# Swapped copies of N and Z taken from GpSimd, masks of P ahead of the weight loads, three unread products fewer, in the begin of a DeltaNet and SwiGLU kernel

## The chip, the cores and the metric

One Trainium2 chip, of which the kernel uses one core. A core has TensorE (PE, matrix products), VectorE (DVE), ScalarE (ACT), GpSimd (POOL) and SyncE (SP, which here issues nearly all DMA transfers). Each runs its own instruction list in order and waits on semaphores for the others. TensorE reads SBUF and writes PSUM.

The metric is the time of one execution on the device in microseconds. The time before is the median of three runs.

## What is computed

The reference first runs a recurrence over 768 steps for each of 4 batches and 8 heads (head size 48), and then a SwiGLU block over the 3072 tokens (model size 384, inner size 1536), all in 32-bit floats:

```python
k_n = k / (np.linalg.norm(k, axis=-1, keepdims=True) + 1e-06)
state = np.zeros((B, H, D, D), dtype=np.float32)
for t in range(S):
    kt, vt, bt = (k_n[:, :, t], v[:, :, t], beta[:, :, t, None])
    y[:, :, t] = np.einsum('bhd,bhde->bhe', q[:, :, t], state)
    v_old = np.einsum('bhde,bhd->bhe', state, kt)
    state = state + bt[:, :, :, None] * np.einsum('bhd,bhe->bhde', kt, vt - v_old)
...
x = np.ascontiguousarray(attn_out.transpose(0, 2, 1, 3)).reshape(B * S, H * D)
g = x @ w_gate
silu = g * (1.0 / (1.0 + np.exp(-g)))
val = x @ w_val
return (silu * val @ w_out).astype(np.float32)
```

## The kernel before

**Chunks.** The 768 steps are cut into 12 chunks of 64. Within a chunk the recurrence is solved with matrices: the products of all keys with all keys (`gram_steps`, `first_gram`), the inverse of a triangular matrix built from them, and the products of queries with keys, P, of which a mask keeps one triangle (`under_mask`, L539). Chunk by chunk the state is passed on, and the 256 tokens of a finished chunk go through the SwiGLU block. Arrays over batch and head are split in two by parity of the head (`par`) and two by batch (`b`); each combination has one half of the 128 partitions, 64 rows. `ORDER` (L360) walks through the four combinations, and matrix products of 64x64 are issued for each.

**The begin.** Chunks 0 and 1 are treated apart. Their triangular matrices are cut into blocks of 16 and 32: VectorE inverts the blocks of 16 by substitution (`first_substitution`, L690, 15 steps of two operations), `first_z` turns the result, and `spread_z` (L714) writes it under a row mask into `ztp[0]`, as the matrix Z: its blocks on the diagonal, one call for each chunk and each half x of the columns (columns 0 to 31 and 32 to 63), on the engine that it is given. Z is thus the inverse of the blocks on the diagonal alone. What stands below them is taken in by N: `n_products` (L728) makes N from the low blocks (`l_sb`) and Z in two PSUM banks, one for each parity, and `n_copies` (L738) copies both banks to SBUF (`n_sb`). It then writes a second copy of the odd parity with the two halves of the partitions swapped (`n_back`, L744), since a product needs its two operands on the same partitions. In the kernel before this copy is made on GpSimd, from SBUF to SBUF, in two parts of 64x512.

**The first chunk.** `first_advance` (L939) is a generator that is stepped by hand. Counted as products for the first chunk, all in L950 and in two parts each (bp 0 in the banks `px`, bp 1 in `py`):

1. Z by V, copied to `v` by ScalarE (L975),
2. N by `v`, copied to `uu` (L985),
3. N by `uu`, with `n_back` as the weights for odd parity; VectorE adds it to `v` in `t` (L997), and ScalarE copies the odd half of `t` to the other partitions (L999),
4. N by `t`, added to `t` in `uu` by VectorE (L1009),
5. the masked P (`p_sb`) by `uu`, copied to `y` (L1022 and L1024, bp 0 on ScalarE, bp 1 on VectorE).

Then `y` is turned on TensorE (L1036) and copied to `x_first` (L1037), which the SwiGLU products of chunk 0 read; and `of_state` (L916) makes the state after chunk 0. Chunk 1 does the same in `advance` (L1111) with its own N (`n_products(1)` at L2019), stepped between the SwiGLU products of chunk 0.

**The weights.** w_gate, w_val and w_out come in 42 pieces; pieces 0 to 23 are 128x256 each, alternately of the gate and the value matrix, six for each 256 inner columns. `stage` (L250) issues the load of one on SyncE's queue. To keep few loads in flight, `stage(n, after)` first lets GpSimd copy one column of piece `after` into the place of piece n (L261, called a gate below): the load of n waits for this copy, and the copy for the landing of piece `after`. A staged piece is then converted to the form in which TensorE reads it: two operations on ScalarE (`power_step`, L274 and L280, called the powers of a piece) and three on VectorE (`convert`, L293, L301, L313). The SwiGLU products of the first chunks are in `gate_val` (L1544); their matrix products are L1552.

**The order.** The engines' instruction lists are exactly in the order in which the program issues the instructions (`manual_schedule`, L1908). The order of the begin is written out from L1917 on. What an engine, or SyncE's queue, has earlier in this list it finishes earlier: a gate that waits for a load holds up everything behind it on GpSimd. `unread(n, bank)` (L634) issues n products of constants whose result nobody reads. `first_q[0]` is the generator of P of chunk 0: its first step makes the products, the second copies them to `p_sb` (ScalarE, L521), and the third and fourth mask one parity each on GpSimd (L536).

In the kernel before GpSimd's list from the first loads on is therefore: the gates of pieces 2 to 7, the swapped copies of N of chunk 0, the gates of 8 and 9, the two masks of P, the gates of 10 to 13, `spread_z` of chunk 1 twice (L1981), the gates of 14 to 17, and the swapped copies of N of chunk 1.

Of the kernel before, what the change touches and what calls it, by code (L numbers as in the profile page):

```python
# [20 lines left out]
def kernel(  # L21
# [25 lines left out]
    nc = tc.nc  # L47
# [25 lines left out]
    def ps_pair(name, tag):  # L73

        return pairs_of_banks[tag]
# [58 lines left out]
    def halves(x, c, b):  # L134
        return x[NB * b : NB * b + NB, :, c * C : (c + 1) * C, :]
# [43 lines left out]
    def load_v(c):  # L179
        vin[c] = work.tile([128, 2, NB, NJ, D], FP32, name="vin", bufs=2)  # L180
        for b in range(2):
            src = halves(v, c, b).rearrange("bp (j par) p d -> par p (bp j) d", par=2)
            for par in range(2):
                s = half_of(b ^ par if c > 1 else b).start
                nc.sync.dma_start(  # L185
                    out=vin[c][s : s + 64, par].rearrange("p bp j d -> p (bp j) d"),
                    in_=src[par],
                )
# [174 lines left out]
    def half_of(x):  # L363
        return slice(64 * x, 64 * x + 64)
# [89 lines left out]
    def banks(name, tag):  # L454

        if type(tag) is int:
            return [ps_ffn([128, 512], name, tag + i) for i in range(2)]
        p = ps_pair(name, tag)
        return [p[:, 0], p[:, 1]]
# [141 lines left out]
    first_of, l_sb, n_sb = {}, {}, {}  # L601
# [32 lines left out]
    def unread(count, p):  # L634

        for _ in range(count):
            nc.tensor.matmul(p[0:R], half, half[:, 0:1].to_broadcast([128, 512]))
# [100 lines left out]
    def n_copies(c, p_n, copies, back):  # L738
        for par in range(2):
            copies[par](  # L740
                n_sb[c][:, par].rearrange("p bp j i -> p (bp j i)"), p_n[par]
            )
        for x in range(2):
            back(n_back[c][half_of(x)], n_sb[c][half_of(1 - x), 1].rearrange(  # L744
                "p bp j i -> p (bp j i)"
            ))

    n_back = {}

# [189 lines left out]
    def first_advance():  # L939

        zt = ztp[0][:, 0].rearrange("p (par bp j) i -> p par bp j i", par=2, bp=NB)
        r = vin.pop(0)
        p_n = banks("p_n", 2)
        n_products(0, p_n)
        n_copies(0, p_n, (nc.scalar.copy, nc.vector.tensor_copy), nc.gpsimd.tensor_copy)

        def product(p, at, flip, weights, moving):
            for j in range(NJ):
                for par, b in ORDER:
                    nc.tensor.matmul(  # L950
                        p[half_of(b ^ par if flip else b), at[par], j],
                        weights(par, b, j),
                        moving(par, b, j),
                    )

        def there(par, b):
            return half_of(b ^ par)

        v, uu = new_u("v0"), new_u("uu")
        t = x_flat.rearrange("p (x bp j d) -> p x bp j d", x=3, bp=NB, j=NJ)  # L960
        pairs = [
            ps_pair("p_u", tag)[:, :, 0 : NJ * D].rearrange("p x (j d) -> p x j d", j=NJ)
            for tag in ("px", "py")
        ]
        n_of = n_sb[0]
        back_of = n_back[0].rearrange("p (bp j i) -> p bp j i", bp=NB, j=NJ)
        for bp in range(NB):
            product(
                pairs[bp],
                (1, 0),  # L970
                True,
                lambda par, b, j: zt[half_of(b), par, bp, j],
                lambda par, b, j: r[half_of(b), par, bp, j],
            )
            nc.scalar.copy(v[:, :, bp], pairs[bp])  # L975
        yield MORE
        for bp in range(NB):
            product(
                pairs[bp],
                (0, 1),  # L980
                False,
                lambda par, b, j: n_of[there(par, b), par, bp, j],
                lambda par, b, j: v[there(par, b), 1 - par, bp, j],
            )
            nc.scalar.copy(uu[:, :, bp], pairs[bp])  # L985
        yield MORE
        for bp in range(NB):
            product(
                pairs[bp],
                (1, 0),  # L990
                True,
                lambda par, b, j: (
                    back_of[half_of(b), bp, j] if par else n_of[half_of(b), 0, bp, j]
                ),
                lambda par, b, j: uu[half_of(b), par, bp, j],
            )
            plus(t[:, 0:2, bp], v[:, :, bp], pairs[bp])  # L997
            for x in range(2):
                nc.scalar.copy(t[half_of(x), 2, bp], t[half_of(1 - x), 0, bp])  # L999
        yield MORE  # L1000
        for bp in range(NB):
            product(
                pairs[bp],
                (0, 1),
                False,
                lambda par, b, j: n_of[there(par, b), par, bp, j],
                lambda par, b, j: t[there(par, b), 1 - par, bp, j],
            )
            plus(uu[:, :, bp], t[:, 1:3, bp], pairs[bp])  # L1009
        held_loads[26] = lambda: load_v(2)  # L1010
        yield
        pq = p_sb.pop(0)
        y = work.tile([128, NB, NJ, 2, D], FP32, name="y", tag="r", bufs=2)
        for bp, copy in enumerate((nc.scalar.copy, nc.vector.tensor_copy)):
            product(
                pairs[bp],
                (0, 1),
                True,
                lambda par, b, j: pq[half_of(b), par, bp, j],
                lambda par, b, j: uu[half_of(b), par, bp, j],  # L1020
            )
            copy(y[:, bp, :, 0], pairs[bp][:, 0])  # L1022
            for b in range(2):
                copy(y[half_of(b), bp, :, 1], pairs[bp][half_of(1 - b), 1])  # L1024
        yield
        y_f = y.rearrange("p bp j par d -> p bp (j par d)")
        xts[0] = x_first
        p_f = [
            p[:, 0 : KT * 128].rearrange("p (t n) -> p t n", t=KT)
            for p in banks("p_f", 2)  # L1030
        ]
        x_v = x_first.rearrange("p t (bp n) -> p t bp n", bp=NB)
        for bp, copy in enumerate((nc.scalar.copy, nc.vector.tensor_copy)):
            for k in range(KT):
                at = slice(k * 128, (k + 1) * 128)
                nc.tensor.transpose(p_f[bp][:, k], y_f[:, bp, at], ident)  # L1036
            copy(x_v[:, :, bp], p_f[bp])  # L1037
        yield
        p_s = of_state(0, uu)
        nc.scalar.copy(state, p_s)  # L1040
        yield
# [581 lines left out]
    def plus(out, a, b):  # L1623
        nc.vector.tensor_tensor(out=out, in0=a, in1=b, op=ALU.add)  # L1624
# [283 lines left out]
    with tc.manual_schedule(  # L1908
# [18 lines left out]
        copy_a = nc.scalar.copy  # L1927
# [14 lines left out]
        for n in range(6):  # L1942
            stage(n, n - 2 if n > 1 else None)
        load_v(1)
        unread(2, banks("p_t", "py")[0])
        turned(2, False, "py")
        first_q = [gram_steps(0, True, 0, (copy_a, copy_a))]
        next(first_q[0])
        gram(2, False, "px", (copy_a, copy_a))
        turned(3, False, "py")  # L1950
        unread(1, banks("p_t", 2)[0])
        turned(1, True, "px")
        gram(3, False, "py", (copy_a, copy_a))
        first_q.append(gram_steps(1, True, "px", (copy_a, copy_a)))
        next(first_q[1])
        next(first_q[0])
        unread(4, banks("p_t", 2)[0])
        first_substitution()
        first_z()
        some, others = slice(0, 1), slice(1, NB)  # L1960
# [4 lines left out]
        scale_v(0)  # L1965
        next(first_q[1])
        stage(6, 4)
        stage(7, 5)
        zb_1 = work.tile([128, R, R], FP32, name="zb", bufs=1)
        new_nt(0, spare_of_q, state_flat[:, LEAD : LEAD + 512])  # L1970
        new_nt(1, zb_1.rearrange("p k i -> p (k i)"), spare_of_q[:, 0:512])
        gens["advance", (0,)] = [first_advance(), 0]
        step("advance", advance, 0)
        for n in (8, 9):
            stage(n, n - 2)
        next(first_q[0])
        next(first_q[0])
        for n in range(10, 14):
            stage(n, n - 3)
        for x in range(2):  # L1980
            spread_z(1, x, nc.gpsimd)  # L1981
        for n in range(14, 23):
            stage(n, n - 3 if n < 18 else None)
        power_step(0)
        step("advance", advance, 0)
        converts_first(0)
# [18 lines left out]
        def chain(_):  # L2005

            at = len(went)
            went.append(1)
            n, ahead = (1, 2, 4, 1, 2, 1, 2, 1, 2, 1, 2, 1)[at], (7, 6, 4, 4)[min(at, 3)]
            if n:  # L2010
                convert(todo[:n], ahead)
                del todo[:n]
            if at in chain_at:
                if at in chain_at[4:6]:
                    next(first_q[1])
                if at == 0:
                    step("advance", advance, 0)
                    p_n = banks("p_n", 2)
                    n_products(1, p_n)  # L2019
                    n_copies(1, p_n, (copy_a, copy_a), nc.gpsimd.tensor_copy)  # L2020
                else:
                    step("advance", advance, 1)

# [74 lines left out]
```

## Time and profile before

| | |
|---|---|
| median of three runs | 671.86 us (670.39 to 671.89) |
| the profiled execution's own time | 672.2 us |
| its span, first to last instruction | 670.5 us |
| TensorE busy (page, part 1) | 651.4 us, 97% |
| VectorE, ScalarE, GpSimd busy | 476.7, 279.1, 208.0 us |
| mean granted clock of TensorE | 0.987 |

The page's part 1 gives busy times and part 2 the span in 40 slices. The timeline lists instructions with start and length in us from the start of the span, merges equal ones that follow each other (x64), and shows in brackets how long the engine stood idle before and what released it. TensorE's instructions overlap in a pipeline, so that lengths of merged rows can overlap. The table of stretches gives busy times, instructions and the granted clock in any cut of the span; the clock is 1.00 or 0.50, and a value between them is a stretch that holds a change. "PEld" is the loading of weights into TensorE, "issue" is time in which an engine waited for nothing that the profile shows.

Some rows of GpSimd and VectorE that the change touches, from the groups by line of the first 60 us:

| operation | mean of one |
|---|---|
| L744 POOL copy 64x512, SBUF to SBUF | 610 ns |
| L740 ACT copy 128x512 from PSUM | 586 ns |
| L740 DVE copy 128x512 from PSUM | 691 ns |
| L540 POOL mask 128x512 | 1350 ns |
| L726 POOL spread of Z 128x512 | 2054 ns |
| L726 DVE spread of Z 128x256 | 437 ns |
| L724 ACT spread of Z 128x256 | 742 ns |

### The profile page before, as it was taken

To read this page: it belongs to the slowest core of one execution; us is meant where nothing else is said; L and a number is where in the kernel's file an instruction comes from. 1 tells how busy PE (TensorE), PEld (TensorE's weight loads), DVE (VectorE), ACT (ScalarE), POOL (GpSimd) and SP (SyncE) were. 2 spreads that over 40 slices of the span, in tenths; PEclk is the share of its full clock that TensorE was granted. 3 is DMA by queue.
4 is the path that set the end of the run, shared out by engine and by line. 5 is a ranking of instruction groups with operands and counts; after the bars stand their busy time and mean duration, and the time that the engine had idled before them with its cause. 6 is when DMAs were issued, how large, how long until landed. Compare 5 with 4: busy or idle time off the path is not lost.

```text
span 670.5 us, 24923 instructions
## 1 busy us (share of the span) xinstructions
PE 651.4 (97%) x10854; PEld 598.6 (89%) x10854; DVE 476.7 (71%) x989; ACT 279.1 (42%) x622; POOL 208.0 (31%) x316
## 2 busy tenths in 40 slices
PE   8859999999999999999999999999999999999997
PEld 4548888856899999999999999999999999999997
DVE  6748979899968867858766857766848655655562
ACT  5646776505432642342542442542332532433330
POOL 7052050105697030883030883030883000000000
PEclk9968999999999999999999999999999999999999
DMA  9565757002861262176364175254164342132221
GB/s 135 128 181 177 239 94 218 2 12 32 250 106 50 47 138 81 31 146 158 64 134 116 28 142 142 63 122 104 35 148 107 79 107 80 52 93 72 73 79 24
DMA packets 147438, 68.57 MB, mean 102 GB/s; under 512 B 123456, under 2 KB 126560, under 8 KB 147328
## 3 DMA queue, kind: packets, MB, share of 16 engines
q1 hardware_dynamic: 144992, 66.48, 41.7%
q8 instruction: 85, 1.39, 0.9%
q10 hardware_dynamic: 2080, 0.39, 0.4%
q0 software_dynamic: 256, 0.10, 0.1%
q14 instruction: 25, 0.20, 0.1%
HBM read 59.08 MB, written 7.86 MB: 100 GB/s over the span
## 4 chain that ended last, share of the span: by engine, by line
PE 83%; DVE 6%; DMA 4%; SPq 3%; ACT 2%; issue 2%; POOL 0%; DVEq 0%; ACTq 0%; POOLq 0%
PE ffn L1397 39%; PE ffn L1671 20%; PE ffn L1581 4%; PE ffn L1552 4%; DMA h_f<-in_moe_w_val_dram 2%; PE p_px L1159 2%; PE p_px L920 2%; SPq L139 1%; PE p_py L1061 1%; PE p_px L1142 1%; PE p_py L501 1%; PE p_py L1078 1%; PE p_px L501 1%; SPq L185 1%; PE p_py L902 1%
## 5 line engine op out<-in xcount | busy, mean ns | idle before, releaser
L1397 PE MATMUL ffn<-x_t,w_gv 128*128 128x128 f32 x800 | 108.7, 279 | 0.8 <-DVE p_sb L1621 0.8
L1397 PEld LDWEIGHTS ffn<-x_t,w_gv 128*128 128x128 f32 x800 | 97.4, 192 | 3.6 <-DVE p_sb L1621 1.3
L1431 ACT ACTIVATE sil<-ffn 128x256 f32<-128x256 f32 x100 | 36.5, 383 | 115.8 <-PE ffn L1397 108.9
L1397 PE MATMUL ffn<-x_ffn,w_gv 128*128 128x128 f32 x640 | 84.6, 275 | 0.0
L1671 PE MATMUL ffn<-wo_sb,h_f 128*128 128x192 f32 x480 | 83.9, 328 | 0.0
L819 POOL TENSOR_TENSOR n_b<-mb,half 128x32 f32<-128x32 f32 x5 | 30.4, 6073 | 161.1 <-DVE mb L555 161.1
L1671 PEld LDWEIGHTS ffn<-wo_sb,h_f 128*128 128x128 f32 x480 | 77.9, 190 | 0.6
L1397 PEld LDWEIGHTS ffn<-x_ffn,w_gv 128*128 128x128 f32 x640 | 78.0, 192 | 0.3
L586 POOL TENSOR_TENSOR h_f<-zb,mb 128x31 f32<-128x31 f32 (+15 forms) x124 | 70.7, 570 | 19.2 <-DVE mb L575 9.7
L592 POOL TENSOR_TENSOR zb<-zb,h_f 128x31 f32<-128x31 f32 (+15 forms) x124 | 70.1, 565 | 9.7
L1397 PE MATMUL ffn<-x_t,h_f 128*128 128x128 f32 x472 | 64.9, 280 | 0.7 <-DMA h_f<-w_s 0.4
L1397 PEld LDWEIGHTS ffn<-x_t,h_f 128*128 128x128 f32 x472 | 57.3, 192 | 2.7 <-issue 0.5
L1432 DVE TENSOR_TENSOR h_f<-sil,ffn 128x256 f32<-128x256 f32 x100 | 39.3, 417 | 23.2 <-ACT sil L1431 23.2
L1093 ACT COPY x_ffn<-p_py 32x256 f32<-32x256 f32 (+3 forms) x108 | 39.4, 365 | 29.1 <-PE p_py L1078 27.3
L1621 DVE TENSOR_TENSOR ffn<-p_sb,ffn 128x512 f32<-128x512 f32 x40 | 27.9, 696 | 27.4 <-PE ffn L1397 26.7
L1624 DVE TENSOR_TENSOR ffn<-ffn,p_sb 128x512 f32<-128x512 f32 x40 | 27.2, 689 | 16.0 <-PE ffn L1397 16.0
L1552 PE MATMUL ffn<-x_t,w_gv 128*128 128x256 f32 x144 | 35.4, 397 | 0.9 <-ACT w_gv L274 0.7
L1671 PE MATMUL ffn<-last_k,h_f 128*128 128x192 f32 x200 | 36.0, 327 | 0.0
L1624 DVE TENSOR_TENSOR o_sb<-o_sb,ffn 128x192 f32<-128x192 f32 x50 | 17.5, 350 | 24.1 <-PE ffn L1671 23.5
L1671 PEld LDWEIGHTS ffn<-last_k,h_f 128*128 128x128 f32 x200 | 32.9, 190 | 0.1
L1552 PEld LDWEIGHTS ffn<-x_t,w_gv 128*128 128x128 f32 x144 | 27.2, 195 | 5.7 <-ACT w_gv L274 1.1
L1552 PE MATMUL ffn<-x_ffn,w_gv 128*128 128x256 f32 x144 | 31.9, 380 | 0.0
(330 smaller groups left out, 1184.5 us busy)
## 6 DMA issues: line engine op xcount, KB each, us to landing
h_f<-w_s SPq DMA_DIRECT2D x81, 256.0 KB, 2.9
more_w<-w_s SPq DMA_DIRECT2D x27, 256.0 KB, 2.7
vin<-in_v_dram SPq DMA_DIRECT2D x48, 96.0 KB, 3.4
out_dram<-o_sb SPq DMA_DIRECT2D x48, 96.0 KB, 2.2
kn<-in_k_dram SPq DMA_DIRECT2D x20, 192.0 KB, 4.7
zt<-in_moe_w_out_dram SPq DMA_DIRECT2D x10, 384.0 KB, 4.6
qpad<-in_q_dram SPq DMA_DIRECT2D x36, 64.0 KB, 3.0
w_s<-h_f SPq DMA_DIRECT2D x7, 256.0 KB, 3.4
```

What stands on the lines that cost most here:

```text
L586: engine.tensor_tensor(out=t_v, in0=zb[:, 0 : j + 1, j : j + 1].to_broadcast([128, j + 1, m]), in1=mb[:, j : j + 1, j + 1 : R].to_broadcas ...
L592: engine.tensor_tensor(out=zb[:, 0 : j + 1, j + 1 : R], in0=zb[:, 0 : j + 1, j + 1 : R], in1=t_v, op=ALU.add,)
L819: nc.gpsimd.tensor_tensor(out=n, in0=mb.rearrange("p j i -> p (j i)")[:, 0 : R * R : R + 1], in1=half, op=ALU.pow,)
L1093: nc.scalar.copy(x_all[at % 128 : at % 128 + rows, at // 128].rearrange("p (bp b i) -> p bp b i", bp=NB, b=2), p[64 * half + lo : 64 * hal ...
L1397: nc.tensor.matmul(p[:, u], w(u), moving, start=start and u == 0, stop=True, skip_group_check=True,)
L1431: nc.scalar.activation(silu_of, p[:, 0:2], ACTF.Silu)
L1432: nc.vector.tensor_tensor(out=h_of(c, PAIRS[r][e % 3], e // 3), in0=silu_of, in1=p[:, 2:4], op=ALU.mult)
L1552: nc.tensor.matmul(ps[name][:, i], w_sb[:, t, (f + i) * 128 : (f + i + 1) * 128], xts[c][:, t], start=(t == 0 and i == 0), stop=(t == KT - 1),
L1581: nc.tensor.matmul(p_o, hs[c, f - f % 2][:, f % 2, bp * 128 : (bp + 1) * 128], wo_sb[:, f], start=(f == 0), stop=(f == FT - 1),)
L1621: nc.vector.tensor_tensor(out=out, in0=a, in1=b, op=ALU.subtract)
L1624: nc.vector.tensor_tensor(out=out, in0=a, in1=b, op=ALU.add)
L1671: nc.tensor.matmul(p[x, part], a(f - f % 2)[:, f % 2], b(f), start=not begun and f == 0, stop=f == FH - 1, skip_group_check=True,)
```

## The change

It does five things, all in the order of the begin.

- The swapped copy of N of chunk 0 is made from the PSUM bank instead of from SBUF, one half on VectorE directly behind the copy of N, the other on ScalarE behind the two copies of `v` (after the first product). `n_copies` takes a pair of copies, and None leaves a half to a later call of the new `swap_n`.
- The swapped copy of N of chunk 1 is made from the PSUM bank too, both halves on ScalarE, behind the copies of N.
- Z of chunk 1 is spread on VectorE (x = 0, behind the sums into `uu` of the first chunk's fourth product) and on ScalarE (x = 1, behind the copies to `x_first`).
- The two masks of P of chunk 0 stay on GpSimd, but go behind the gates of piece 6 and of piece 7; all gates and loads up to piece 22 follow directly, ahead of the first chunk's products in the program.
- Three unread products are taken away: one of two before `turned(2)`, the one before `turned(1, True)`, one of four before the substitution ends.

```diff
@@ n_copies
         for x in range(2):
-            back(n_back[c][half_of(x)], n_sb[c][half_of(1 - x), 1].rearrange(
-                "p bp j i -> p (bp j i)"
-            ))
+            if back[x] is not None:
+                swap_n(c, p_n, x, back[x])
+
+    def swap_n(c, p_n, x, copy):
+        copy(n_back[c][half_of(x)], p_n[1][half_of(1 - x)])
@@ first_advance
-        n_copies(0, p_n, (nc.scalar.copy, nc.vector.tensor_copy), nc.gpsimd.tensor_copy)
+        to = nc.vector.tensor_copy
+        n_copies(0, p_n, (nc.scalar.copy, to), (to, None))
...
             nc.scalar.copy(v[:, :, bp], pairs[bp])
+        swap_n(0, p_n, 1, nc.scalar.copy)
         yield MORE
...
             plus(uu[:, :, bp], t[:, 1:3, bp], pairs[bp])
+        spread_z(1, 0, nc.vector)
...
             copy(x_v[:, :, bp], p_f[bp])
+        spread_z(1, 1, nc.scalar)
         yield
@@ the order of the begin
-        unread(2, banks("p_t", "py")[0])
+        unread(1, banks("p_t", "py")[0])
         turned(2, False, "py")
...
         turned(3, False, "py")
-        unread(1, banks("p_t", 2)[0])
         turned(1, True, "px")
...
-        unread(4, banks("p_t", 2)[0])
+        unread(3, banks("p_t", 2)[0])
         first_substitution()
...
         stage(6, 4)
+        next(first_q[0])
         stage(7, 5)
+        next(first_q[0])
+        for n in range(8, 10):
+            stage(n, n - 2)
+        for n in range(10, 18):
+            stage(n, n - 3)
+        for n in range(18, 23):
+            stage(n)
         zb_1 = work.tile([128, R, R], FP32, name="zb", bufs=1)
...
         step("advance", advance, 0)
-        for n in (8, 9):
-            stage(n, n - 2)
-        next(first_q[0])
-        next(first_q[0])
-        for n in range(10, 14):
-            stage(n, n - 3)
-        for x in range(2):
-            spread_z(1, x, nc.gpsimd)
-        for n in range(14, 23):
-            stage(n, n - 3 if n < 18 else None)
         power_step(0)
...
-                    n_copies(1, p_n, (copy_a, copy_a), nc.gpsimd.tensor_copy)
+                    n_copies(1, p_n, (copy_a, copy_a), (copy_a, copy_a))
```

## The prediction

> **What bounds the kernel now.** Page part 1 has TensorE busy for 651.4 of 670.5 us. Its waits from 120 us to the end add up to 1.9 us, and between 51.1 and 120 us it has none, so what the change can move lies in the begin. There I read TensorE's row of the timeline from 27 us on: start, length, what runs, and in brackets the idle time before it with what ended it.
>
> ```profile
> 27.96 1.16 PE L734 MATMUL ffn<-zt,a_sb 64*64 64x64 f32 x64
> 32.23 0.61 PE L950 MATMUL p_px<-v,qpad 64*64 64x48 f32 x27 [1.45 <-issue]
> 33.46 0.31 PE L950 MATMUL p_px<-uu,qpad 64*64 64x48 f32 x2
> ...
> 38.21 0.34 PE L950 MATMUL p_px<-uu,state 64*64 64x48 f32 x1 [4.44 <-POOL state L744]
> ...
> 40.05 1.10 PE L950 MATMUL p_px<-x_t,qpad 64*64 64x48 f32 x32
> 44.61 0.68 PE L950 MATMUL p_px<-uu,p_sb 64*64 64x48 f32 x32 [2.61 <-DVE uu L1624]
> 46.37 1.76 PE L1036 MATMUL ffn<-ident,y 128*128 128x128 f32 x6 [0.36 <-ACT y L1024]
> 48.88 3.41 PE L1552 MATMUL ffn<-x_t,w_gv 128*128 128x256 f32 x6 [0.74 <-ACT w_gv L274]
> ```
>
> The third product of the first chunk starts at 33.46 and stands still after two matmuls until 38.21, for the swapped copy of N (L744). The fifth waits for `uu`. From 48.88 on the FFN products fill TensorE. Why the copy is late stands in GpSimd's row, and why `uu` is late in VectorE's:
>
> ```profile
> 35.97 0.18 POOL L261 COPY h_f<-h_f 128x1 uint32<-128x1 uint32 x1 [2.84 <-DMA h_f<-in_moe_w_gate_dram]
> 36.65 0.18 POOL L261 COPY h_f<-h_f 128x1 uint32<-128x1 uint32 x1 [0.50 <-DMA h_f<-in_moe_w_val_dram]
> 36.90 1.26 POOL L744 COPY state<-qpad 64x512 f32<-64x512 f32 x2
> ...
> 41.05 2.67 POOL L540 TENSOR_TENSOR p_sb<-p_sb,mask_q 128x512 f32<-128x512 f32 x2
> ```
> ```profile
> 41.08 1.51 DVE L301 SCALAR_TENSOR_TENSOR w_gv<-w_gv,h_f 128x256 uint32<-128x256 uint32 x1
> 42.63 1.37 DVE L313 CUSTOM_DVE_ANT_0 w_gv<-w_gv,last_h 128x512 uint16<-128x512 uint16 x1
> ```
>
> N has been in SBUF since 29.96 (the VectorE copy L740: 29.27 + 0.69); its swapped copies stand in GpSimd's queue behind the gates of pieces 6 and 7, which wait for pieces 4 and 5 to land. The masks of P follow at 41.05 and run beside a conversion of VectorE whose two operations take 1.51 and 1.37 us; both take 0.42 at 31.94 and 32.40, with GpSimd still.
>
> Last the clock, from the table of busy times cut at its changes (stretch; then length, busy us and count of PE, PEld, DVE, ACT, POOL; granted clock, DMA share, GB/s):
>
> ```profile
> 28.27:31.68 3.41, 2.32 (x128) 1.96 (x119) 1.58 (x3) 2.70 (x7) 0.79 (x1) 1.00 0.51 156
> 31.68:35.09 3.41, 1.45 (x62) 1.20 (x61) 1.07 (x3) 1.59 (x4) 0.37 (x2) 1.00 0.47 135
> 35.09:38.50 3.41, 0.29 (x12) 0.29 (x15) 0.00 (x0) 0.00 (x0) 1.59 (x4) 0.50 0.73 149
> ...
> 45.33:48.74 3.41, 2.45 (x37) 1.52 (x28) 1.64 (x5) 3.14 (x10) 1.84 (x2) 0.50 0.76 241
> 48.74:52.15 3.41, 3.13 (x6) 1.67 (x6) 3.31 (x6) 2.61 (x9) 3.41 (x5) 0.50 0.18 64
> 52.15:55.57 3.42, 3.42 (x125) 3.36 (x128) 3.32 (x11) 1.89 (x4) 0.56 (x2) 0.50 0.72 222
> ```
>
> The clock changes only at steps of 3.41 us. A stretch 68% busy kept it whole, one 42% busy was followed by half, stretches of 72 and 92% at half clock did not raise it, and a full one did (at 55.57).
>
> **The change, part by part**, on the times of this execution.
>
> *Unread products.* Three fewer at 3.63/4 = 0.91 us each. The product N at 27.96 starts 0.13 after the ScalarE spread (27.09 + 0.74), which ends VectorE's substitution chain. VectorE sets this start, and no unread product feeds it: worth 0 (at most 0.1 gained). The cover gone is the clock's: rival 2.
>
> *Swapped copies of chunk 0.* GpSimd loses 2 x 0.61. VectorE gets one, as long as L740's 0.69 at most and L1024's 0.36 (64x192) at least; I take 0.69: 29.96 to 30.65, with only conversion 0 behind it. ScalarE gets the other after `v` (30.88): 0.59 at most (L740), 0.32 at least (L1024): done at 31.5. Behind it the powers of piece 0 end at 32.3 instead of 31.53, before the `uu` copies that wait for TensorE (32.93). Conversion 0 on VectorE then ends at 33.6, before it is wanted at 34.2. So the third product no longer stops: 33.46 to about 34.6.
> The 1.45 us of "issue" before 32.23 I leave; if it goes, the third product comes earlier still, and the masks below decide all the same.
>
> *From the third to the fifth product.* Sum into `t`: 34.2 to 35.3 (two L1624 of 0.55). Fourth product 34.8 to 36.05. Conversion 2, between on VectorE (0.28 + 0.42 + 0.42 with gaps): to 36.6 alone, to 38.1 if both long operations are stretched again. Then `uu`: first half at 37.2 to 38.7.
>
> *Masks.* On GpSimd now: gate 6 at 35.97 to 36.15 (piece 4 lands when it did; nothing ahead of it changes), mask 0 for 1.35, gate 7 for 0.2, mask 1 for 1.35: done at **39.05**. The fifth product needs both, so it starts near 39.1; `uu` comes 0.4 to 1.9 sooner and sets nothing. What is late next: gate 7 goes from 36.65 to 37.5, so piece 7's load from 37.49 to 37.7.
>
> *Spreading Z of chunk 1.* GpSimd loses 4.1 us (47.06 to 51.1). VectorE gets 128x512 after `uu`: 0.7 to 0.87 from L726's 0.437 for 256 columns, 2.05 (GpSimd's own row) if stretched: done before the `y` copy at 41.1. ScalarE gets the other after x: twice L724's 0.742 at most, 0.74 at least; I take 1.2. The powers behind it (pieces 3 and 5) come near 44 and are converted after 47. Gone too is the stretching of piece 4's conversion (0.61 and 1.26 at 48.6; 0.28 and 0.42 otherwise).
>
> *Loads.* All ahead of GpSimd's long work: piece 10 goes out near 41.3 instead of 44.07, 14 near 47 instead of 51.95, 18 near 50.7 instead of 55.90. That is 3 to 5 us earlier; ScalarE took 14 4 us after landing. Enough for a move by 6.
>
> *Swapped copies of chunk 1.* ScalarE gets 2 x 0.59 after L740, ahead of SiLU: SiLU 0.7 and the powers of pieces 11 to 13 about 1 us later within the chain; VectorE wanted power 11 4 us after it was made. 0.
>
> *The sum.* From the fifth product to the FFN the row shows 48.88 - 44.61 = 4.27, partly at half clock. After the change the stretch 35.09 to 38.50 holds only the fourth product, about 1.0 us (30%), so the fifth is at half clock too (+0.4): the FFN starts at 39.1 + 4.7 = 43.8, which is **5.1** earlier. Its half clock then lasts until 48.74 (45.33 to 48.74 is full), 4.9 us instead of 6.7: half of 1.8 is **0.9** more. 5.1 + 0.9 = **6.0 us**, and after that neither engine has a time of its own to wait for: VectorE still has its 2.66 us of slack before L1150. Span 670.5 - 6.0 = 664.5. The profiled execution took 672.2 (1.7 around the span), 0.3 above the median shown, 671.86; so the forecast is 671.86 - 6.0 = **665.9**, by itself 664.4 to 667.6 (`uu` later than the mask, one clock step either way).
>
> **Rivals.**
>
> 1. *The clock stays whole.* Its steps may fall elsewhere in another execution. If the gap after the fourth product (36.05 to 39.1) is shared by two stretches, neither is as empty as 42%: the FFN starts whole, 0.4 + 4.9/2 = 2.9 more: 663.0. For: the gap is shorter than a stretch; against: the waits at 40 to 43 follow close. Chance 0.12.
> [...]
>
> 2. *The clock falls before 28 us,* for want of unread products. 14.62 to 18.03 holds 3.09 busy now and about 2.2 without the first, 64%: near the 68% that kept the clock. If it falls and comes back only after the last three, these cost up to 6 x 0.86 (the first rows of L637) instead of 2.7, and the products behind start about 3 us late, of which the masks hide 0.4 to 1.9; with products at half clock some 1 to 3.5 are lost: 667 to 669.4, I take 668. Chance 0.11.
> [...]
>
> 3. *VectorE or the loads give it back.* The conversions of pieces 6, 8, 10 end at 62.97, and TensorE wants them at 63.11: 0.14 of slack, on an engine busy 9.86 of 10 us there. If a later power or load holds them, TensorE waits: 4 to 6 us given back, 670 to 672. Against: this stretch begins with L1150, which TensorE itself releases. Chance 0.10.
>
> 4. *It doesn't do what it says:* the third or fifth product finds another wait of the same place (piece 4 landing later, or another stop like the one before 32.23). Two such waits of 1.45 leave 669. Chance 0.04.
>
> 5. *Slower.* The half clock isn't left. Each stretch after 48.74 with over about 0.28 us idle (8%, as in 48.74 to 52.15) keeps it and costs 1.7 us of work. The gain of 6.0 is gone with the fourth, at 62.4; with the fifth, at 65.8, it is 2.5 slower: 674.4. For: with copies added to ScalarE the products of chunk 1 could wait between FFN products. Against: no wait from 51.06 to 120. Chance 0.08.
>
> **How the numbers follow.** Forecast 0.55, rivals 0.12, 0.11, 0.10, 0.04, 0.08. The range 663.0 to 669.5 holds the forecast and rivals 1, 2 and 4, and leaves out 3 and 5, 0.18. A measurement here tells 0.3% (2 us) from no change: faster is below 669.8. Forecast and rivals 1, 2, 4 make 0.82; rival 3 is the same, 0.10; rival 5 slower, 0.08.
>
> **What would show it.** TensorE's row without the wait for L744, third product near 33.5 and whole; the fifth released by GpSimd's L540 near 39.1; first L1552 near 43.8; half clock from 38.5 to 48.7; piece 14's load before 48. Wrong it would be if TensorE waits anew between 45 and 80 us, if the clock falls before 28, or if the fifth product still starts after 42.

## The result and the profile after

The changed kernel takes 666.46 us (median of four runs, 665.16 to 667.19); the kernel before took 671.47 us (four runs) beside it. The ratio is 0.9926, with a 95% interval from 0.9905 to 0.9946: 5.0 us faster, where 6.0 were forecast. The profiled execution took 666.14 us with a span of 664.4, against 672.2 and 670.5 before: 6.1 us less.

The changed kernel's timeline of TensorE, in the columns used before (start, length, what runs, idle time ahead and what ended it). Its lines lie a little lower: L953 is L950 of before, L1041 is L1036, L1558 is L1552, L1630 (the sums on VectorE) is L1624.

```profile
28.13 1.16 PE L734 MATMUL ffn<-zt,a_sb 64*64 64x64 f32 x64 [1.49 <-ACT zt L724]
...
33.33 0.25 PE L953 MATMUL p_px<-uu,qpad 64*64 64x48 f32 x1
33.34 0.25 PE L953 MATMUL p_px<-uu,state 64*64 64x48 f32 x1
...
34.76 0.43 PE L953 MATMUL p_px<-x_t,qpad 64*64 64x48 f32 x10 [0.28 <-DVE x_t L1630]
...
37.03 0.28 PE L953 MATMUL p_px<-uu,p_sb 64*64 64x48 f32 x2 [0.35 <-DVE uu L1630]
37.62 0.62 PE L953 MATMUL p_px<-uu,p_sb 64*64 64x48 f32 x27 [0.31 <-POOL p_sb L540]
...
39.37 1.53 PE L1041 MATMUL ffn<-ident,y 128*128 128x128 f32 x6 [0.61 <-ACT y L1029]
41.64 2.90 PE L1558 MATMUL ffn<-x_t,w_gv 128*128 128x256 f32 x6 [0.74 <-ACT zt L724]
```

The third product no longer stops. The fifth starts with `uu` and then, after two matrix products, waits 0.31 us for the second mask. The first FFN product starts at 41.64 instead of 48.88, 7.2 us earlier. GpSimd's timeline shows why the second mask was late:

```profile
33.35 0.18 POOL L261 COPY h_f<-h_f 128x1 uint32<-128x1 uint32 x1 [0.42 <-DMA h_f<-in_moe_w_gate_dram]
33.49 1.46 POOL L540 TENSOR_TENSOR p_sb<-p_sb,mask_q 128x512 f32<-128x512 f32 x1
35.91 0.42 POOL L261 COPY h_f<-h_f 128x1 uint32<-128x1 uint32 x1 [0.97 <-DMA h_f<-in_moe_w_val_dram]
36.29 1.27 POOL L540 TENSOR_TENSOR p_sb<-p_sb,mask_q 128x512 f32<-128x512 f32 x1
```

Piece 4 had landed by 33.35 in this execution, 2.6 us sooner than in that of before, and the gate of piece 7 held mask 1 until piece 5 landed. The clock, in the table of stretches (length, busy us and count of PE, PEld, DVE, ACT, POOL, granted clock, DMA share, GB/s):

```profile
32.98:36.40 3.42, 2.57 (x141) 2.19 (x132) 2.94 (x8) 3.03 (x9) 2.08 (x4) 1.00 0.45 114
36.40:39.81 3.41, 2.14 (x84) 1.66 (x76) 2.57 (x6) 1.99 (x7) 1.16 (x1) 1.00 0.62 109
39.81:43.22 3.41, 2.59 (x8) 1.84 (x8) 2.35 (x6) 3.41 (x9) 0.69 (x3) 0.50 0.59 201
43.22:46.64 3.42, 3.42 (x84) 2.68 (x86) 3.28 (x11) 2.22 (x7) 0.64 (x2) 0.50 0.74 237
46.64:50.05 3.41, 3.41 (x131) 2.85 (x123) 0.87 (x3) 3.37 (x8) 0.55 (x3) 1.00 0.65 201
```

Half clock lasts for two steps of 3.41 us, from 39.81 to 46.64; before it lasted for five (35.09 to 41.91 and 45.33 to 55.57).

**Where the time went after that.** The first product of chunk 1 with the state (L1142, now L1148) starts at 48.95 instead of 57.23: 8.3 us ahead. Not all of this arrives:

```profile
56.32 0.79 PE L1192 MATMUL p_px<-v,zb 64*64 64x48 f32 x37
57.75 0.66 PE L1192 MATMUL p_px<-v,zb 64*64 64x48 f32 x27 [0.65 <-issue]
```

The kernel before has no such stop at this place:

```profile
64.60 1.15 PE L1186 MATMUL p_px<-v,zb 64*64 64x48 f32 x64
```

The stop takes 0.9 (it stands in two later profiles of the changed kernel too, with 1.27 and 0.72 us of idle time), and the thirty FFN products at 71.42 lie 7.3 us ahead of those at 78.76. The lead stays at 7.4 to 126.59 (L1587; 134.03 before), and between 300 and 400 us it falls to 6.1; 0.7 of this is one wait of an FFN product for the reload of summed weights from DRAM (L1397, now L1403), 1.1 us against 0.4 in the kernel before. In the twelve profiles of the experiments below, too, the lead over this one profile of before shrinks between the first product of chunk 1 with the state and the end of the span, by 0.6 (j_three_parts, 6.8 to 6.2) to 4.1 us (g_after, 7.8 to 3.7); a_swap0 is 3.5 us ahead there and 1.0 at the end. How far ahead a single profile is in the begin says only roughly what the kernel gains.

### The profile page after: what moved, and what is told of

Read it like the earlier page. It is cut to its first block, busy times and chain, and to the rows that moved or that the text cites. A ratio compares the mean times of both kernels' runs of the same rounds, so it can differ in the third digit from the quotient of the medians.

```text
span 664.4 us, 24913 instructions
## 1 busy us (share of the span) xinstructions
PE 647.5 (97%) x10848; PEld 596.3 (90%) x10848; DVE 474.8 (71%) x991; ACT 281.6 (42%) x626; POOL 198.0 (30%) x310
## 4 chain that ended last, share of the span: by engine, by line
PE 84%; DVE 9%; DMA 3%; SPq 2%; issue 1%; ACT 1%; POOL 0%; DVEq 0%; POOLq 0%
PE ffn L1403 40%; PE ffn L1677 20%; PE ffn L1558 9%; DMA h_f<-in_moe_w_val_dram 2%; PE p_px L1165 2%; SPq L139 2%; PE p_py L501 1%; PE p_px L922 1%; PE p_py L1067 1%; DVE x_t L586 1%; DVE zb L592 1%; PE p_py L1084 1%; PE p_px L1148 1%; PE p_px L501 1%; PE ffn L1587 1%
## 5 line engine op out<-in xcount | busy, mean ns | idle before, releaser
L1403 PE MATMUL ffn<-x_t,w_gv 128*128 128x128 f32 x800 | 108.7, 279 | 0.8 <-DVE p_sb L1627 0.8
L1403 PEld LDWEIGHTS ffn<-x_t,w_gv 128*128 128x128 f32 x800 | 97.4, 192 | 3.8 <-DVE p_sb L1627 1.6
L1403 PE MATMUL ffn<-x_ffn,w_gv 128*128 128x128 f32 x640 | 84.8, 275 | 0.0
L1403 PEld LDWEIGHTS ffn<-x_ffn,w_gv 128*128 128x128 f32 x640 | 78.0, 192 | 0.4
L821 POOL TENSOR_TENSOR n_b<-mb,half 128x32 f32<-128x32 f32 x5 | 27.6, 5519 | 161.3 <-DVE mb L555 161.3
L1403 PE MATMUL ffn<-x_t,h_f 128*128 128x128 f32 x472 | 64.8, 280 | 1.5 <-DMA h_f<-w_s 1.1
L1403 PEld LDWEIGHTS ffn<-x_t,h_f 128*128 128x128 f32 x472 | 57.3, 192 | 3.5 <-DVE ffn L1630 1.7
L1630 DVE TENSOR_TENSOR ffn<-ffn,p_sb 128x512 f32<-128x512 f32 x40 | 27.2, 689 | 16.7 <-PE ffn L1403 16.7
L1558 PE MATMUL ffn<-x_t,w_gv 128*128 128x256 f32 x144 | 35.0, 396 | 0.7 <-ACT zt L724 0.7
L1630 DVE TENSOR_TENSOR o_sb<-o_sb,ffn 128x192 f32<-128x192 f32 x50 | 17.5, 350 | 24.1 <-PE ffn L1677 23.7
L1558 PE MATMUL ffn<-x_ffn,w_gv 128*128 128x256 f32 x144 | 31.9, 380 | 0.0
L1558 PEld LDWEIGHTS ffn<-x_t,w_gv 128*128 128x128 f32 x144 | 27.3, 196 | 5.0 <-ACT zt L724 1.1
```

The costliest lines, as they stand in the source:

```text
L821: nc.gpsimd.tensor_tensor(out=n, in0=mb.rearrange("p j i -> p (j i)")[:, 0 : R * R : R + 1], in1=half, op=ALU.pow,)
L1403: nc.tensor.matmul(p[:, u], w(u), moving, start=start and u == 0, stop=True, skip_group_check=True,)
L1558: nc.tensor.matmul(ps[name][:, i], w_sb[:, t, (f + i) * 128 : (f + i + 1) * 128], xts[c][:, t], start=(t == 0 and i == 0), stop=(t == KT - 1),
```

## The experiments

The kernels fall into three groups (a to d, e to i, j to m); each shares one chip and its own runs of the kernel before, whose median was 672.67, 672.10 and 670.51 us. "Ratio" is to those runs (for the first row of the changed kernel, to the four of the result), with the 95% interval. The last four columns come from each one's profile: start of the fifth product and of the first FFN product, total time at half clock up to 60 us, span.

| kernel | median us | ratio | fifth | FFN | half clock | span |
|---|---|---|---|---|---|---|
| before | (above) | 1 | 44.61 | 48.88 | 17.1 | 670.5 |
| changed | 666.46 | 0.9926 [0.9905, 0.9946] | 37.03 | 41.64 | 6.8 | 664.4 |
| a_swap0 | 671.51 | 0.9987 [0.9965, 1.0008] | 40.35 | 46.39 | 13.7 | 669.5 |
| b_masks | 672.45 | 0.9983 [0.9961, 1.0004] | 44.08 | 48.92 | 17.1 | 671.1 |
| c_swap0_masks | 671.44 | 0.9981 [0.9959, 1.0002] | 39.65 | 44.48 | 23.9 | 669.8 |
| d_unread_back | 668.18 | 0.9937 [0.9913, 0.9961] | 39.12 | 43.60 | 10.2 | 667.1 |
| g_after (changed) | 667.87 | 0.9923 [0.9894, 0.9952] | 38.57 | 42.92 | 6.8 | 666.8 |
| e_no_unread | 668.39 | 0.9951 [0.9924, 0.9978] | 38.46 | 43.30 | 17.1 | 666.2 |
| f_masks_first | 666.79 | 0.9920 [0.9899, 0.9941] | 37.38 | 41.05 | 3.4 | 663.8 |
| i_fill | 665.51 | 0.9908 [0.9883, 0.9933] | 37.85 | 42.59 | 6.8 | 664.0 |
| m_after (changed) | 667.69 | 0.9943 [0.9922, 0.9964] | 39.11 | 43.94 | 13.7 | 665.9 |
| j_three_parts | 666.58 | 0.9929 [0.9908, 0.9951] | 38.81 | 43.65 | 13.7 | 664.3 |
| k_masks_early | 667.69 | 0.9947 [0.9924, 0.9970] | 38.93 | 42.60 | 3.4 | 663.7 |
| l_early_fill | 665.37 | 0.9904 [0.9880, 0.9928] | 38.33 | 42.00 | 3.4 | 664.0 |

### One part of the change alone, and two

a_swap0: the kernel before with the swapped copy of N of chunk 0 as in the change.

```diff
-        n_copies(0, p_n, (nc.scalar.copy, nc.vector.tensor_copy), nc.gpsimd.tensor_copy)
+        to = nc.vector.tensor_copy
+        n_copies(0, p_n, (nc.scalar.copy, to), (to, None))
...
+        swap_n(0, p_n, 1, nc.scalar.copy)
```

> The kernel before with one part of the change: the swapped copy of N of chunk 0 on VectorE and ScalarE; the masks of P stay behind the gates of pieces 8 and 9. Theory (the fifth product is bound by the masks as soon as the third no longer waits, so that the two moves are worth something only together): the third product starts near 33.4, but the fifth waits for GpSimd's masks, which come at 41 to 43.7 as before; it starts 0.5 to 1.5 us earlier than in the kernel before, and the time falls by 0.5 to 1.5 us. Rival (the wait for the swapped copy is the whole loss and the masks have slack): fifth product near 39, time 4 to 5 us less.

It took 671.51 us, 1.2 less, which its interval doesn't tell from nothing. TensorE's row, and GpSimd's:

```profile
40.35 0.44 PE L958 MATMUL p_px<-uu,p_sb 64*64 64x48 f32 x2 [2.52 <-POOL p_sb L540]
41.57 0.99 PE L958 MATMUL p_px<-uu,p_sb 64*64 64x48 f32 x27 [0.78 <-POOL p_sb L540]
```
```profile
38.90 0.18 POOL L261 COPY h_f<-h_f 128x1 uint32<-128x1 uint32 x1 [0.45 <-DMA h_f<-in_moe_w_val_dram]
39.04 2.48 POOL L540 TENSOR_TENSOR p_sb<-p_sb,mask_q 128x512 f32<-128x512 f32 x2
```

The fourth product starts at 34.81, 5.2 us sooner than before, and the fifth then stands until the masks end, in two pieces of 2.5 and 0.8 us: the wait changed its place. The loads were early in this execution (gate 9 at 38.90 instead of 40.76), so the masks came earlier than I expected and the FFN 2.5 us sooner.

b_masks: the kernel before with the masks behind the gates of 6 and 7, the swapped copy on GpSimd behind them.

```diff
         stage(6, 4)
+        next(first_q[0])
         stage(7, 5)
+        next(first_q[0])
...
-        next(first_q[0])
-        next(first_q[0])
```

> The kernel before with one part of the change: the two masks of P behind the gates of pieces 6 and 7; the swapped copy of N stays on GpSimd, directly behind them. Theory: the third product now waits for gate, masks and copies in a row, some 2 us later than before; the fifth no longer meets a conversion that is stretched by the masks, some 2 us sooner after the third; the time changes by less than 1.5 us either way. Rival (the masks alone carry the gain): time 3 us less or better.

672.45 us, 0.2 less: as expected. The third product waits 6.6 us for L744 instead of 4.4, the fourth begins at 41.64 instead of 40.05, and the fifth at 44.08.

c_swap0_masks: these two edits together.

> The kernel before with those two parts together, and nothing else: Z of chunk 1 is still spread on GpSimd behind the gate of piece 13, N of chunk 1 still swapped there, the unread products all there. Theory: the two together give the gain of the change, 4.5 to 6.5 us. Rival (the loads that come earlier, or the unread products, carry half of it): 2 to 3 us.

My theory fell: 671.44 us, 1.2 less, no more than the first part alone. The fifth product did come 5 us sooner (39.65) and the FFN 4.4 (44.48). Then, in its timeline of TensorE and of GpSimd:

```profile
47.30 1.96 PE L927 MATMUL p_px<-uu,kn 64*64 64x48 f32 x64
51.15 1.98 PE L734 MATMUL ffn<-zt,a_sb 64*64 64x64 f32 x64 [1.88 <-POOL zt L726]
```
```profile
46.30 0.26 POOL L261 COPY wo_sb<-wo_sb 128x1 uint32<-128x1 uint32 x1
46.54 4.55 POOL L726 TENSOR_SCALAR zt<-mb,m_rows 128x512 f32<-128x512 f32 x2
```

N of chunk 1 needs Z of chunk 1, which GpSimd still spreads behind the gate of piece 13. In the kernel before the spread ended at 51.1 and TensorE came for it at 54; now TensorE comes at 49. And its clock did not recover (the stretches cut at the steps, columns as above):

```profile
46.89:50.30 3.41, 2.37 (x66) 1.80 (x64) 3.31 (x7) 1.83 (x4) 3.41 (x2) 0.50 0.50 154
50.30:53.71 3.41, 2.56 (x66) 2.36 (x67) 1.60 (x6) 0.53 (x2) 1.65 (x4) 0.50 0.40 111
53.71:57.13 3.42, 3.42 (x51) 2.50 (x52) 0.00 (x0) 1.65 (x5) 1.40 (x3) 0.50 0.83 259
```

The wait of 1.9 us lies across two stretches and keeps both below full (70 and 75%), and the half clock goes on through them and through the next, which is full. The state after chunk 0 (L927) is 4.9 us ahead of before, N of chunk 1 behind the wait 2.8, and L1151, the first product of chunk 1 with the state, at 55.92, only 1.3. This is the mechanism of rival 5, in a kernel that has two of the change's parts. The other runs of this kernel agree in the mean: the granted clock over the span is 0.981 to 0.992 in the twelve, median 0.987, where the kernel before beside it has a median of 0.985 and the changed kernel, in its three measurements, 0.989 to 0.998.

j_three_parts: c with the spread as in the change, the new hypothesis alone.

```diff
-        for x in range(2):
-            spread_z(1, x, nc.gpsimd)
...
             plus(uu[:, :, bp], t[:, 1:3, bp], pairs[bp])
+        spread_z(1, 0, nc.vector)
...
             copy(x_v[:, :, bp], p_f[bp])
+        spread_z(1, 1, nc.scalar)
```

> The kernel before with three parts: the swapped copy of N of chunk 0 off GpSimd, the masks behind the gates of pieces 6 and 7, and Z of chunk 1 spread on VectorE and ScalarE. N of chunk 1 is still swapped on GpSimd and the unread products are all there. The two parts without the third had given 1 us: GpSimd's spread of Z then ended at 51.1 and TensorE waited 1.9 us for it, at half clock until 57.1. Theory (the spread is the third thing that GpSimd holds up, and the half clock that goes with its wait is the rest): no wait for the spread, half clock gone by 50, time 4 to 6 us less than the kernel before, as the whole change. Rival (the swapped copies of chunk 1 or the unread products matter too): 2 us less at most.

666.58 us, 3.9 less than the kernel before; the changed kernel beside it (m_after) took 667.69. N of chunk 1 follows the state after chunk 0 (L927) at once, at 47.86, and half clock ends at 47.4. The mean granted clock of its six runs is 0.990 to 0.992, median 0.9905; against the 0.987 of c_swap0_masks this is worth some 2.3 us of work at full clock (an estimate: 0.0035 of a span of 665), of the 2.7 by which their gains differ. As far as these runs tell, the three parts are the whole gain, and the swapped copies of chunk 1, the earlier place of the loads in the program and the unread products together make no difference that shows. Its 3.9 lies a little under my 4 to 6, and m_after's 2.8 clearly so; this group's runs of before have the lowest median of the three groups.

### The unread products

d_unread_back: the changed kernel with 2, 1 and 4 unread products as before.

> The changed kernel with the three unread products put back. Theory: VectorE's substitution chain sets the start of N, so that they cost nothing: same time as the changed kernel within 0.7 us, N's products again near 28. Rival (TensorE was late for N, and taking them away gave time): 1 to 2.7 us more than the changed kernel. Rival (they keep the clock): 1 to 2 us less.

Ratio 0.9937 [0.9913, 0.9961], against 0.9926, 0.9923 and 0.9943 for the three measurements of the changed kernel: no difference. N starts at 28.19, as in the changed kernel (28.13).

e_no_unread: none at these three places.

```diff
-        unread(1, banks("p_t", "py")[0])
         turned(2, False, "py")
...
-        unread(3, banks("p_t", 2)[0])
         first_substitution()
```

> The changed kernel without the unread products that it keeps behind the first four products of keys: none before the third chunk's keys are turned, none before the substitution ends (the change left 1 and 3). Theory (the last three keep the clock, since TensorE would stand still from 24 to 28 us): half clock before or at N's products, N's and V's products at half speed, 1 to 3.5 us more than the changed kernel. Rival (a gap of 4 us there falls into two stretches of 3.41 us and the masks hide what it costs): within 0.7 us of the changed kernel.

> The changed kernel again, as a measure for the runs beside it. 4 to 6 us less than the kernel before; half clock for two or three steps of 3.41 us between 32 and 50 us, where the steps fall anew in each execution.

The first half of the theory held, the second didn't. The clock fell twice before 30 us:

```profile
12.30:15.71 3.41, 1.51 (x19) 1.03 (x11) 3.04 (x6) 3.32 (x11) 1.41 (x1) 1.00 1.15 146
15.71:19.13 3.42, 3.42 (x76) 3.09 (x79) 2.90 (x13) 2.79 (x9) 0.50 (x1) 0.50 0.93 159
25.95:29.37 3.42, 1.18 (x67) 1.07 (x67) 3.28 (x6) 1.78 (x4) 0.56 (x3) 1.00 0.49 155
29.37:32.78 3.41, 3.41 (x122) 3.41 (x124) 1.36 (x2) 2.37 (x5) 0.85 (x3) 0.50 0.59 159
```

The stretches 44 and 35% busy were each followed by half clock; the mean clock of its ten runs is 0.982 to 0.994, against 0.991 to 0.998 in g_after. But 668.39 us against 667.87 of the changed kernel beside it is 0.5 us, inside both spreads. The products of V and N at half speed (1.11 us for 32 matmuls of the first product, 0.68 in g_after) run through the stop of 1.3 us that the changed kernel has inside its second product (32.59 in g_after), and N does not start later (28.04).

### Masks earlier still, and a fuller TensorE

f_masks_first: both masks ahead of the gate of piece 6.

```diff
+        next(first_q[0])
+        next(first_q[0])
         stage(6, 4)
-        next(first_q[0])
         stage(7, 5)
-        next(first_q[0])
```

> The changed kernel with both masks of P ahead of the gate of piece 6, which waits for piece 4 to land (33.4 in the changed kernel's profile, 36.0 in that of the kernel before). Theory (the masks behind these gates set the fifth product where the loads come late, and the sums into uu where they come early): the fifth product is released by VectorE's uu in every execution, 0.3 to 2 us earlier, and the time falls by 0.3 to 2 us. Rival (masks beside VectorE's conversion of piece 0 and the sums into t stretch these, or gates 6 and 7 come later and hold loads): same or up to 2 us more.

0.9920 against 0.9923: the same. The fifth product is released by `uu` as foreseen, but `uu` is late, since the masks (33.02 to 35.71) now run beside VectorE's conversion of piece 0:

```profile
32.60 0.42 DVE L301 SCALAR_TENSOR_TENSOR w_gv<-w_gv,h_f 128x256 uint32<-128x256 uint32 x1
33.06 1.51 DVE L313 CUSTOM_DVE_ANT_0 w_gv<-w_gv,h_f 128x512 uint16<-128x512 uint16 x1
34.60 0.55 DVE L1630 TENSOR_TENSOR x_t<-v,p_px 128x384 f32<-128x384 f32 x1
```

L313 takes 1.51 us, the sum into `t` waits for VectorE, and the fourth product stands 1.1 us. This is not new with the edit: in g_after and m_after the first mask also began 0.04 us ahead of L313, which took 1.52; in the first profile of the changed kernel L313 began 0.11 us ahead of the mask and took 0.42. So there was little left to gain. The sums themselves take 0.55 beside the second mask; in the kernel before, with no mask beside them, they took 0.56 and 0.55 (39.44 and 40.29).

k_masks_early: both masks between the gates of pieces 3 and 4.

```diff
-        for n in range(6):
+        for n in range(4):
             stage(n, n - 2 if n > 1 else None)
-        load_v(1)
...
         next(first_q[0])
+        next(first_q[0])
+        next(first_q[0])
+        for n in range(4, 6):
+            stage(n, n - 2)
+        load_v(1)
```

> The changed kernel with both masks of P between the gates of pieces 3 and 4, near 28.5 to 31, when VectorE copies N from PSUM and no conversion or sum into t runs. Theory (masks first, at 33.0 to 35.7, met the sums into t, of which the fourth product then stood 1.1 us waiting, and that ate the gain): sums into t end near 35.2, uu near 37, fifth product within 0.4 us of the fourth, 0.5 to 1.5 us less than the changed kernel. Rival (gate 4 waits for the masks and piece 4 and all later loads come 1 us later; or the scaling of V is stretched): same or up to 1 us more.

667.69 us, as m_after, with the widest spread of all (663.57 to 671.54 in twelve runs). I had misjudged what the masks would meet. In its profile they ran from 27.61 to 30.25, and VectorE's spread of Z of chunk 0 stood there:

```profile
27.62 3.22 DVE L726 TENSOR_SCALAR zt<-mb,m_rows 128x256 f32<-128x256 f32 x3
```

These three took 1.15 us in the changed kernel. They release N, whose second half starts at 30.89. What the masks cost differed with what of VectorE they lay beside (L313 1.51 us instead of 0.42, three L726 3.22 instead of 1.15, the sums 0.55 as without them), and neither of the two earlier places is better than that of the change.

i_fill is f_masks_first, and l_early_fill is k_masks_early, each with two added products of constants that nobody reads, of 256 columns.

```diff
                 copy(y[half_of(b), bp, :, 1], pairs[bp][half_of(1 - b), 1])
+        unread(1, ffn_banks[0][:, 0:256])
         yield
...
             copy(x_v[:, :, bp], p_f[bp])
+        unread(1, ffn_banks[0][:, 0:256])
```

> The kernel with the masks first, and two more unread products of 256 columns: one behind the fifth product, while y is copied, one behind the turning of y, while x is copied. Theory (the half clock after 39.8 comes from a stretch 65% busy, and two steps of it cost half of 6.8 us): the stretches are over three quarters busy, the clock stays whole or is half for one step fewer, and the time falls by 1.5 to 3 us against the masks first alone. Rival (turning y does not count as busy, or the stretch is still too empty): half clock for as long as before, 0 to 0.6 us more for the added products.

> The same with the two added products of 256 columns behind the fifth product and behind the turning of y. Theory (a fuller TensorE keeps the clock from falling after 36, or brings it back a step sooner): half clock for one step of 3.41 us or none, 1 to 3 us less than the changed kernel. Rival (where the steps fall decides, not these products): within 0.7 us of the kernel without them.

> The changed kernel once more, as a measure for the runs beside it: 4 to 6 us less than the kernel before.

i_fill took 665.51 us, f_masks_first 666.79; l_early_fill took 665.37, k_masks_early 667.69. Both differences have the expected sign, and neither is clear of its intervals. The profile of i_fill missed its expectation: its clock fell at 34.44, ahead of the added products, and was half for two steps, one more than in that of f_masks_first. But each of the six runs of l_early_fill (663.72 to 666.32) is below each of the six of the changed kernel beside it (666.51 to 668.26). It has the lowest median here, hardly below that of i_fill, and is 0.9904 [0.9880, 0.9928] of the kernel before. Its stretches from 32.66 on:

```profile
32.66:36.08 3.42, 3.42 (x127) 3.36 (x128) 1.50 (x5) 1.92 (x5) 0.54 (x2) 0.50 0.65 183
36.08:39.49 3.41, 2.44 (x129) 2.17 (x126) 3.09 (x7) 2.26 (x8) 0.18 (x1) 1.00 0.77 170
39.49:42.90 3.41, 3.09 (x14) 1.49 (x14) 2.60 (x8) 3.37 (x9) 0.77 (x3) 1.00 0.34 94
```

39.49 to 42.90, with nearly all of both added products in it (they run at 39.41 and 41.19), is 91% busy and keeps the clock, so that the first FFN product runs whole (six matrix products in 1.73 us, against 2.90 in the changed kernel). In k_masks_early the clock stayed whole there too, without them (67% busy). The runs together say more than the two profiles, since each has its mean granted clock: 0.996 or 0.997 in all six of l_early_fill, but 0.983 to 1.000 in the twelve of k_masks_early, of which only four reach 0.996; 0.994 to 0.997 in i_fill, 0.991 to 0.997 in f_masks_first. So the added products go with a steadier clock. That they alone make the 2.3 us is not shown: in the profile of l_early_fill the masks ran from 29.20, with three operations of VectorE beside them that took 1.61 us in all (29.25 to 32.66), and N started at 27.98 instead of 29.27.

## Why the prediction was right, and where it was not

The direction, the place and the total held: 666.5 us against 665.9, inside the range. By its steps:

- **Third product.** Foreseen near 33.46 and whole, came at 33.33. That the stop of "issue" ahead of it stays was right too (1.05 us).
- **The masks set the fifth product.** 39.05 was foreseen, with piece 4 landing when it did before. It landed 2.6 us earlier, and the fifth came at 37.0 to 37.6, by `uu` and the mask at once. In the two other profiles of the changed kernel the masks ended at 36.3 and 36.5, `uu` at 38.4 and 39.0, and `uu` decided. So the step that `uu` "sets nothing" failed: in one profile of three the mask stopped the fifth product after `uu` had started it, and in two `uu` alone set it. There the first mask, earlier than foreseen, began beside conversion 0 (L313 1.52 us instead of the 0.42 reckoned with), and the fourth product ran at half clock at least in part (in g_after 1.15 us for 30 of its matmuls, against 0.65 for 32 in f_masks_first). The start of the FFN, foreseen at 43.8, came at 41.6, 42.9 and 43.9. a_swap0 shows the mask as the next wait behind the swapped copy, as argued.
- **The spread of Z** was the term that I mis-sized. I costed the move on VectorE and ScalarE and a stretched conversion, and asked nowhere what a spread left on GpSimd would delay once TensorE came 5 us sooner. c_swap0_masks shows the price: two moves without it bring 1.2 us, three bring 3.9. It did no harm to the sum only because the change moves it.
- **Half clock** was to last 4.9 us beyond the start of the FFN; it lasted 5.0 (41.64 to 46.64). But it was foreseen from 38.5 to 48.7, with the fifth product in it, and came from 39.81 to 46.64, with the fifth product whole; that the two lengths agree is partly chance. The gain from it (0.9 foreseen) was right in kind: by 48.95 the lead was 8.3, of which 7.2 at the FFN's start.
- **"After that neither engine has a time of its own to wait for"** failed. 0.9 us went at the stop near 57, a new wait between 45 and 80 us of the kind that the prediction named as a sign of being wrong, and 1.3 between 300 and 400. A lead 2.3 us larger than foreseen and 2.2 lost later make the 6.1 of the profile, so part of its closeness to 6.0 is chance.
- **Unread products** at 0: d_unread_back agrees. **Swapped copies of chunk 1** at 0: ScalarE's SiLU came at 50.32 behind them, and nothing on TensorE waited; j_three_parts, which leaves them on GpSimd, agrees.
- **Loads.** Pieces 10, 14 and 18 went out at 42.35, 47.58 and 53.04 (foreseen 41.3, 47 and 50.7), and no FFN product waited for one.
- **Rivals.** The clock did not stay whole in the changed kernel (1), though its half time was 6.8, 6.8 and 13.7 us in three profiles. Its early fall (2) happened in e_no_unread and cost nothing that shows (0.5 us, inside the spreads), not 1 to 3.5; it also came, at 13.1 and 13.3 us, in k_masks_early and in j_three_parts, which has all the unread products. VectorE (3) kept pace: its wait for L1148 is 2.73 us, as 2.66 before. A stop like the one before 32.23, of which rival 4 spoke, came at 57, and a shorter one (0.46) inside the fourth product. Rival 5 did not come in the changed kernel, but in c_swap0_masks.

Whether turning (the products with `ident`) counts as busy for the clock, which a rival in the expectation of i_fill raises, the profiles settle only in part. In k_masks_early a stretch 75% busy was followed by half clock, and the next, full, by the whole clock:

```profile
9.66:13.07 3.41, 2.56 (x83) 1.88 (x82) 1.90 (x5) 2.16 (x5) 3.41 (x2) 1.00 1.25 176
13.07:16.48 3.41, 3.41 (x10) 1.55 (x10) 3.24 (x7) 2.65 (x9) 0.65 (x1) 0.50 1.22 151
```

In the changed kernel 9.09 to 12.51, as busy (2.56 us, of which 1.15 were turning), kept the clock, and so did 7.79 to 11.21 in the kernel before (2.56 us with 1.09 of turning). The changed kernel's 12.51 to 15.92 kept it with 2.52 us, of which 1.54 were turning, where 29.82 to 33.23 of c_swap0_masks, 1.65 us busy without any turning, was followed by half clock. Apart from turning that kept stretch held some 1.0 us, less than the 1.65 that did not keep it; so I take turning to count at least in part (an estimate from these stretches). Why the clock fell early in k_masks_early and j_three_parts stays open.

## What to carry to other kernels

When a queue in order holds several things that others wait for behind one slow wait, taking out the first shows the second, and then the third: list all of them, with the time at which each is wanted once the others are gone, before pricing any one move. Here each of two moves alone was worth nothing that could be told, both together no more (1.2 us, not clear of nothing), and all three about 4. And a wait on TensorE can cost more than itself: behind the one of 1.9 us in c_swap0_masks the clock stayed at half, and the lead fell by 3.6 us.

## What the runs showed of the hardware

- The clock's steps fell elsewhere in each execution. In the fourteen profiles the first fall after the start lay between 13.1 (k_masks_early) and 41.8 us (f_masks_first), and the time at half clock up to 60 us between 3.4 and 23.9 us. For three profiles of the same kernel it was 6.8, 6.8 and 13.7. The share of a stretch in which TensorE was busy does not tell by itself whether the clock fell after it. Half clock followed stretches 35 and 44% busy (e_no_unread), 42% (31.68 to 35.09 before), 50% (l_early_fill, 29.25 to 32.66), 63% (36.40 to 39.81 of the changed kernel) and 75% (k_masks_early, 9.66 to 13.07). The whole clock stayed after 52 and 75% (26.16 to 29.57 and 32.98 to 36.40 of the changed kernel), 68% (28.27 to 31.68 before) and 72% (l_early_fill, 36.08 to 39.49). It came back after full stretches (at 41.91 and 55.57 before, 46.64 in the changed kernel, 57.13 in c_swap0_masks), and not after one of 92% (48.74 to 52.15 before) or two of 94 and 90% (c_swap0_masks, 33.23 to 36.65 and 40.06 to 43.47).
- Beside GpSimd's masks and spreads some of VectorE's operations took longer: L313 1.51 us instead of 0.42 (f_masks_first), three L726 3.22 instead of 1.15 (k_masks_early), L301 1.51 and 1.27 instead of 0.42 (before, at 41.08 and 49.28). L301 and L313 of the kernel before, which began at 41.08 and 42.63 while a mask ran, ended 0.3 us after that mask (42.60 and 44.00; the masks at 42.31 and 43.72), and L726 of the changed kernel 0.5 after its (38.03 and 37.56). Sums with one operand in PSUM (L1630, 0.55 us) took the same beside a mask, and some ended before it did (36.88 in the changed kernel, the mask at 37.56).
- The same load landed at different times: piece 4 had landed by 33.4 or 36.0 us in two profiles with the same instructions ahead of it on the queue, and the gate that waited for it began at 33.35 and 35.97.
